# A planned order with later places, and another beginning: induced attention and a squared-ReLU layer on one core

## The chip, the cores and the metric

The kernel runs on one core of a Trainium2 chip. The metric is the device time of one execution in microseconds (us); the time before is the median of three runs. TensorE (PE) multiplies and transposes, ScalarE (ACT) and VectorE (DVE) work on what it leaves in PSUM and in SBUF, GpSimd (POOL) does some elementwise steps, and SyncE (SP) issues every DMA.

## What is computed

The input `x` has 4 batches of 12480 rows of 128 numbers, `inducing` 32 rows of 128. The two weights are float64: 128 x 2048 and 2048 x 128.

```python
def mab(q, kv):
    s = scale * (q @ kv.transpose(0, 2, 1))
    s = s - s.max(-1, keepdims=True)
    a = np.exp(s)
    a /= a.sum(-1, keepdims=True) + 1e-09
    return a @ kv
h = mab(I, x)                     # 32 inducing rows look at a whole batch
x2 = mab(x, h).reshape(-1, 128)   # each row looks at the 32 results
h = np.maximum(x2 @ w_in, 0.0)
out = h * h @ w_out
```

## The kernel before, in words

A batch is cut into 13 units of 960 rows (`NU`), a unit into two blocks of 480 columns (`BLK`); there are 52 units. Three kinds of work exist.

**First** (class `First`, L356) is the first attention of one unit: load it (L369), transpose it on PE (`xtp`, L388) and copy it to `xt`, scores against the inducing rows (`score`, L403), maximum and running shift on DVE (L416, L422), exponential on ACT (L429, L432), transpose the weights of the attention (`ep`, L437) and copy them to `et`, multiply with `xn` (`mix`, L457), and add up the running sum (`hacc` L469, `zs` L479). `first_end` (L509) closes a batch: it joins four groups of lanes into `hT`, multiplies it with the first weight in four pieces (`wp`, L559), and splits that into `hw` (L563, L568).

**Second** (L590) is the second attention of a unit: scores (`na`, L599), copy (`ss`), transpose (`s2t`, L616), maximum and subtraction (L623, L627), exponential (L630), a high and a low part `sk` (L649, L653), sum and reciprocal square (L634, L637, L640, L644: the last gives `zz`), transpose back (`ap`, L660), copy (`sw`) and four DMAs that spread it (`st<-sw`, L675).

**The layer** (`ffn_block`, L734) runs over quads of four 128-wide slices of the hidden size: four products `h` (L755) into two PSUM tiles of two banks, two ReLUs (L763) into `g`, one square (L774), a high part `hi` (L778) and a low part `lo` (L782) on DVE, and twelve products into `op` (L795). A unit has 8 quads, so 32 products `h` and 96 products `op`. At the end of a block `op` is copied (`ot`), transposed (`otp`, L815), scaled by `zz` (L823) and, for each unit, stored.

The weights come as float64 words in eight chunks of 512 KB (`weights`, L235; four of the first weight, `i0` to `i3`, four of the second, `o0` to `o3`). A chunk goes through `clamp` (L254, DVE), `size` (L260, ACT), `flush` (L263), `field` (L267), `sign` (L273), `power` (L279), `low` (L283, all DVE); then a chunk of the first weight has one sum on POOL (L322), one of the second a copy on ACT (L339) and two steps on POOL (L343, L344).

The order of all this is not written by hand. `Plan.run` (L66) is a list scheduler: each task has an engine, an assumed duration, a due time and needs; a task may start when its needs have ended plus `LATENCY` of the engine that did them, and when its buffers are free (their last user's end plus 60 ns, L98). Among tasks that could start within 40 ns of the engine's being free, the one due first is taken (L112). The plan sets only the order in which each engine's instructions are emitted: on the chip each engine runs its queue in that order and waits for semaphores where it must. SP's loads are ordered in the same way. The first batch has all 13 units of `First` done ahead of the layer, with no layer to hide behind (L846 to L857); in the other batches `First`, `Second` and the layer of different units are mixed. The task `opened` (L856) opens the memory of `g`, `hi` and `lo` where the weights' and the first units' tiles were; all ReLUs of unit 0 need it.

Of the kernel before, what the change touches and what calls it, by code (L numbers as in the profile page):

```python
# [20 lines left out]
P = 128  # L21
TS = 120
# [5 lines left out]
class Task:  # L28
    def __init__(self, engine, ns, fn, due, needs, port, mode, takes, order):
        self.engine, self.ns, self.fn, self.due = engine, ns, fn, due  # L30
        self.needs, self.port, self.mode, self.takes, self.order = needs, port, mode, takes, order
        self.start = self.end = self.ready = None
        self.waiting = 0
        self.then = []
# [9 lines left out]
class Plan:  # L44
# [7 lines left out]
    LATENCY = {"PE": 220.0, "ACT": 150.0, "DVE": 150.0, "POOL": 150.0, "SP": 2500.0}  # L52
    SWITCH = 95.0

    def __init__(self, room):
        self.room, self.tasks = room, []

    def add(self, engine, ns, fn, due, needs=(), port=False, mode=None, takes=(), reads=()):

        t = Task(engine.split("|"), ns, fn, due, [n for n in needs if n is not None], port, mode, takes, len(self.tasks))  # L60
        for b in list(takes) + list(reads):
            b.users.append(t)
        self.tasks.append(t)
        return t

    def run(self):  # L66
# [20 lines left out]
        def room_at(t):  # L87
            at = 0.0
            n = {}
            for b in t.takes:  # L90
                n[b.tag] = n.get(b.tag, 0) + 1
                old = taken.get(b.tag, [])
                i = len(old) + n[b.tag] - 1 - self.room[b.tag]
                if i >= 0:
                    for u in (old[i].users if i < len(old) else ()):
                        if u.end is None:
                            return None
                        at = max(at, u.end + 60.0)  # L98
            return at
# [42 lines left out]
def induced_attention_then_squared_relu_ffn(  # L142
# [19 lines left out]
    PERIOD, START, T_MAIN, NARROW, STEP = 32000.0, 2600.0, 66000.0, 6000.0, 1700.0  # L162
    W_DUE = [8000.0 + 6500.0 * k for k in range(8)]

    XT, OT, ST, SKH = ("ACT|DVE", "ACT|DVE"), ("ACT|DVE", "ACT|DVE"), "ACT|DVE", "ACT|DVE"
# [11 lines left out]
    plan = Plan(dict(xn=3, early=6, xt=NU + 1, m=2, h=2, o=2, g=GB, hi=HB, lo=LB, st=2, sw=2, words=2))  # L177
# [54 lines left out]
    LEAST = float(np.array(897 << 20, np.int32).view(np.float32))  # L232
    ABOVE = float(np.array(1151 << 20, np.int32).view(np.float32))

    def weights(name, load, use, due):  # L235

# [15 lines left out]
        def clamp():  # L252
            v["hc"] = tile_of("hc", F32)
            nc.vector.tensor_scalar(  # L254
                v["hc"], v["w"][:, :, 1].bitcast(F32), ABOVE, -ABOVE, ALU.min, ALU.max
            )

        def size():
            v["m"] = tile_of("m", F32)
            nc.scalar.activation(v["m"], v["hc"], AF.Abs)  # L260

        def flush():
            nc.vector.scalar_tensor_tensor(v["hc"], v["m"], LEAST, v["hc"], ALU.is_ge, ALU.mult)  # L263

        def field():
            v["a"] = tile_of("a", I32)
            nc.vector.tensor_scalar(  # L267
                v["a"], v["hc"].bitcast(I32), 3, 0x3FFFFFF8,
                ALU.logical_shift_left, ALU.bitwise_and,
            )  # L270

        def sign():
            nc.vector.scalar_tensor_tensor(  # L273
                v["a"], v["hc"].bitcast(I32), -0x40000000, v["a"], ALU.bitwise_and, ALU.bitwise_or
            )

        def power():
            v["power"] = tile_of("m", I32)
            nc.vector.tensor_single_scalar(v["power"], v["a"], -0x800000, ALU.bitwise_and)  # L279

        def low():
            v["b"] = tile_of("b", F32)
            nc.vector.scalar_tensor_tensor(  # L283
                v["b"], v["w"][:, :, 0].bitcast(U32), 2.0 ** -52, v["power"].bitcast(F32),
# [15 lines left out]
    def open_stage():  # L300
        pools["scope"] = ExitStack()
        pools["early"] = pools["scope"].enter_context(tc.tile_pool(name="early", bufs=6))
        pools["stage"] = pools["scope"].enter_context(tc.tile_pool(name="stage", bufs=2))

    def open_ffn():

        pools["scope"].close()
        pools["ffn"] = ctx.enter_context(tc.tile_pool(name="ffn", bufs=3))

    def load_weights(due):  # L310
# [3 lines left out]
        for k in range(n):  # L314
# [5 lines left out]
            def use(v, needs, due, kw, sl=sl):  # L320
                def join():
                    nc.gpsimd.tensor_add(w_in_sb[:, sl], v["a"].bitcast(F32), v["b"])  # L322

                return add("POOL", 1100, join, due, needs, **kw)

            ins.append(weights(f"i{k}", load, use, due[k]))
        for k in range(n):
# [6 lines left out]
            def use(v, needs, due, kw, k=k):  # L334
# [6 lines left out]
                def rest():  # L341
                    a = v["a"].bitcast(F32)
                    nc.gpsimd.tensor_sub(a, a, hi)  # L343
                    nc.gpsimd.tensor_add(lo, a, v["b"])  # L344
# [11 lines left out]
    class First:  # L356
        def __init__(self, b, u, due, early=False):

            self.b, self.u, self.early, self.n = b, u, early, f"{b}_{u}"
# [11 lines left out]
            loaded = add("SP", 2000, load, due - lead - (4000 if early else 20000), takes=[self.bx])  # L371
# [4 lines left out]
        def turn(self, k, due, loaded):  # L376
# [18 lines left out]
            t = add("PE", 420, turn, due, [loaded] + self.turned,  # L395
# [89 lines left out]
    def first_alone(f, due):  # L485

        v = {}
        bank_s, bank_h = Buffer("h"), Buffer("m")

        def score():  # L490
            v["sp"] = ps_h.tile([P, 2, 512], F32, tag="h", name=f"sp_{f.n}")[:, 0, :2 * TS]
            f.score(v["sp"])

        t = add("PE", 560, score, due, f.turned, mode="n", takes=[bank_s], reads=[f.bt])
        f.weigh(t, lambda: v["sp"], bank_s, due)
        mix_alone(f, due + 4000)

# [11 lines left out]
    def first_end(b, due, step):  # L509
# [46 lines left out]
        def wide(k):  # L556
            sl = slice(k * 512, (k + 1) * 512)
            v["wp", k] = bank(f"wp_{b}_{k}")
# [23 lines left out]
        for k in range(F // 512):  # L582
            bw = Buffer("m")
# [6 lines left out]
    class Second:  # L590
# [13 lines left out]
        def weigh(self, scored, where, bank_, due, step):  # L604
# [31 lines left out]
            def norm1():  # L636
                nc.vector.tensor_scalar_add(v["z"], v["z"], 1e-9)  # L637

            def norm2():
                nc.vector.reciprocal(v["z"], v["z"])  # L640

            def norm3():
                s["zz", u] = tiny.tile([TS, G, 1], F32, tag="zz", name=f"zz_{n}")
                nc.vector.tensor_mul(s["zz", u], v["z"], v["z"])  # L644


            def high():
                v["sk"] = att.tile([TS, Q, 2, 2, M], F32R, tag="sk", name=f"sk_{n}")
                copy(th, v["sk"][:, :, :, 0, :], v["d"].rearrange("t (k q) m -> t q k m", q=Q))  # L649
# [33 lines left out]
            d = due  # L683
            te = add("DVE", 317, evict, d, [scored], reads=[bank_])
# [4 lines left out]
            th = add(SKH, (300, 250), high, d + 3 * step, [tp], port=True)  # L689
            tl = add("DVE", 335, low, d + 3 * step, [th], port=True)  # L690
            t = add("DVE", 330, total, d + 4 * step, [tp])
            t = add("DVE", 75, norm1, d + 5 * step, [t])
            t = add("DVE", 113, norm2, d + 5 * step, [t])
            self.zz = add("DVE", 198, norm3, d + 5 * step, [t])
# [4 lines left out]
    def narrow(second, f, g, due, step, begun=None):  # L699

        v = {}
        bank_a = Buffer("m") if second or f else None
# [9 lines left out]
        def go():  # L712
            if bank_a:
# [20 lines left out]
    def ffn_block(b, u, k, second, t0, first_needs):  # L734
# [7 lines left out]
        def quad(j, last):  # L742
# [4 lines left out]
            for i in range(2):  # L747
# [12 lines left out]
                def relu(i=i, c=c):  # L760
                    if i == 0:
                        v["g"] = pools["ffn"].tile([P, 4, BLK], F32, tag="g", name=f"g_{n}_{j}", bufs=GB)
# [4 lines left out]
                t = add("PE", 217, lambda wide=wide: wide(0), d, need, takes=[bh], reads=[second.bst])  # L767
                w.setdefault("begun", t)
                t = add("PE", 217, lambda wide=wide: wide(1), d, [t], reads=[bh, second.bst])
                relus.append(add("ACT", 855, relu, d + 1000, [t] + first_needs + relus,  # L770
# [5 lines left out]
            def high():  # L776
                v["hi"] = pools["ffn"].tile([P, 4, BLK], F32R, tag="hi", name=f"hi_{n}_{j}", bufs=HB)
                nc.vector.tensor_copy(v["hi"], v["g"])  # L778

            def low():  # L780
                v["lo"] = pools["ffn"].tile([P, 4, BLK], F32R, tag="lo", name=f"lo_{n}_{j}", bufs=LB)
                nc.vector.tensor_sub(v["lo"], v["g"], v["hi"])  # L782

            sq = add("ACT", 1696, square, due + 4000, relus, reads=[bg])
            th = add("DVE", 1070, high, due + 5700, [sq], port=True, takes=[bhi], reads=[bg])
            tl = add("DVE", 2076, low, due + 7800, [th], port=True, takes=[blo], reads=[bg, bhi])
            for m, (wo, name, from_, buf) in enumerate((
                (wo_hi, "hi", th, bhi), (wo_lo, "hi", th, bhi), (wo_hi, "lo", tl, blo),
            )):
                for i in range(2):  # L790
# [10 lines left out]
                    last = add("PE", 434, products, due + 8000 + 600 * (2 * m + i), [from_, last, w_outs[j]],  # L801
# [32 lines left out]
        td = add(OT[k], (455, 570), done, end + 1000, [last], reads=[bo])  # L834
# [14 lines left out]
    t_end = 6000 + START * NU + 4000  # L849
# [3 lines left out]
    firsts[NU] = First(1, 0, t_main)  # L853
    narrow(seconds[0], None, None, t_end + 4000, 800)
    after_stage = w_ins + w_outs + [firsts[NU - 1].summed]
    opened = add("POOL", 1, open_ffn, t_main, after_stage)  # L856
    narrow(None, firsts[NU], None, t_main, 2000)  # L857
    open_stage()
    for w, (b, u) in enumerate(units):
        t_u = t_main + w * PERIOD  # L860
        begun = [ffn_block(b, u, k, seconds[w], t_u + k * PERIOD / 2, [opened] if w == 0 else []) for k in range(2)][0]
# [50 lines left out]
```

## Time and profile before

| | before |
|---|---|
| median of 3 runs | 1776.12 us (1775.27 to 1777.15) |
| the profiled execution's own time | 1777.57 us |
| its span, first to last instruction | 1775.8 us |
| mean granted clock of TensorE | 0.993 |
| busy share of PE, DVE, ACT, POOL | 98%, 92%, 93%, 1% |

The busy shares are averages over two very different parts: a beginning of some 72 us in which only the first attention of batch 0 and the weights are done, and a long part in which the layer runs. A row of the timeline has start, duration, engine, line, operation, out<-in, shape and count, and in brackets the idle time ahead of it with what ended it. The chain of waits lists, in order of time, what each stretch of the span was spent on, followed back from the last instruction.

### The profile page before, as it was taken

What the parts mean: (1) busy time and instruction counts of PE and PEld (TensorE: products, weight loads), DVE (VectorE), ACT (ScalarE), POOL (GpSimd) and SP (SyncE); (2) the same over time, 40 slices, a digit from 0 to 9 for tenths busy, and PEclk for the clock granted to TensorE, in tenths of its full rate; (3) what the DMA queues carried; (4) which work ended last, traced back from release to release, by engine and by line L of the source; (5) the groups of instructions that cost most, each with busy time, mean ns of one, the idle gap of its engine ahead of it and who ended that gap; (6) DMA issues with size and microseconds to landing.
All of it is one profiled execution on the core that took longest, in us unless ns stands there. A gap on an engine that the chain in (4) does not pass through costs nothing.

```text
span 1775.8 us, 24582 instructions
## 1 busy us (share of the span) xinstructions
PE 1736.6 (98%) x9625; PEld 1415.7 (80%) x9625; DVE 1641.0 (92%) x1736; ACT 1652.7 (93%) x1765; POOL 22.2 (1%) x22
## 2 busy tenths in 40 slices
PE   7799999999999999999999999999999999999998
PEld 4488888888788888888888888888887788888886
DVE  6799999999999999999999999999999998999988
ACT  6699999999999999999999999999999999999997
POOL 1200000000000000000000000000000000000000
PEclk9899999999999999999999999999999999999999
DMA  9211211211121211211211211111101001010110
GB/s 234 62 45 45 56 34 45 56 35 44 34 56 45 56 37 43 56 45 36 59 29 45 56 45 38 52 46 48 31 23 42 26 23 45 23 45 23 35 33 23
DMA packets 33532, 82.48 MB, mean 46 GB/s; under 512 B 5032, under 2 KB 20424, under 8 KB 33416
## 3 DMA queue, kind: packets, MB, share of 16 engines
q1 hardware_dynamic: 33416, 80.91, 17.4%
q8 instruction: 76, 1.25, 0.3%
q14 instruction: 40, 0.33, 0.1%
HBM read 29.77 MB, written 25.56 MB: 31 GB/s over the span
## 4 chain that ended last, share of the span: by engine, by line
PE 67%; ACT 20%; issue 9%; DVE 2%; DMA 1%; SPq 0%; ACTq 0%; DVEq 0%
PE op L795 43%; PE h L755 15%; ACT g L763 13%; ACT g L774 6%; PE otp L815 2%; PE xtp L388 1%; PE ap L660 1%; PE na L599 1%; DMA xn<-in_x_dram 1%; PE wp L559 1%; PE s2t L616 1%; PE na L403 1%; DVE lo L782 1%; PE ep L437 1%; ACT xt L224 1%
## 5 line engine op out<-in xcount | busy, mean ns | idle before, releaser
L782 DVE TENSOR_TENSOR lo<-g,hi 128x1920 fp32r<-128x1920 f32 x416 | 895.6, 2153 | 13.0 <-DVE hi L778 0.9
L763 ACT ACTIVATE g<-h 128x960 f32<-128x960 f32 x832 | 783.0, 982 | 47.8 <-PE h L755 42.1
L774 ACT ACTIVATE g<-g 128x1920 f32<-128x1920 f32 x416 | 759.4, 1826 | 5.1
L755 PE MATMUL h<-st,hw 128*128 128x480 f32 x1664 | 644.3, 388 | 15.4 <-ACT g L763 12.5
L778 DVE CAST hi<-g 128x1920 fp32r<-128x1920 f32 x416 | 480.1, 1154 | 78.8 <-ACT g L774 75.3
L795 PE MATMUL op<-lo,wo_hi 128*128 128x480 f32 x1664 | 511.1, 389 | 0.3 <-DVE lo L782 0.3
L795 PE MATMUL op<-hi,wo_lo 128*128 128x480 f32 x1664 | 506.0, 390 | 0.0
L795 PE MATMUL op<-hi,wo_hi 128*128 128x480 f32 x1664 | 481.8, 382 | 0.2 <-DVE hi L778 0.2
L755 PEld LDWEIGHTS h<-st,hw 128*128 128x128 f32 x1664 | 314.3, 189 | 108.3 <-ACT g L763 55.7
L795 PEld LDWEIGHTS op<-hi,wo_hi 128*128 128x128 f32 x1664 | 311.4, 188 | 50.3 <-DVE hi L778 0.9
L795 PEld LDWEIGHTS op<-hi,wo_lo 128*128 128x128 f32 x1664 | 299.6, 188 | 50.6 <-issue 11.7
L795 PEld LDWEIGHTS op<-lo,wo_hi 128*128 128x128 f32 x1664 | 302.2, 189 | 40.4 <-issue 2.7
L224 ACT COPY ot<-op 128x480 f32<-128x480 f32 x99 | 55.8, 564 | 27.1 <-PE op L795 26.9
L823 DVE TENSOR_TENSOR osb<-otp,zz 120x512 f32<-120x512 f32 x104 | 71.2, 684 | 4.2 <-PE otp L815 2.5
L388 PE MATMUL xtp<-ident,xn 120*128 120x120 f32 x416 | 62.7, 278 | 7.3 <-DMA xn<-in_x_dram 5.4
L388 PEld LDWEIGHTS xtp<-ident,xn 120*128 120x128 f32 x416 | 51.0, 147 | 21.0 <-issue 6.2
L815 PE MATMUL otp<-ident,ot 128*120 128x128 f32 x416 | 62.4, 272 | 0.6 <-ACT ot L224 0.6
L815 PEld LDWEIGHTS otp<-ident,ot 128*120 128x120 f32 x416 | 48.9, 137 | 15.6 <-ACT ot L224 6.6
L224 ACT COPY xt<-xtp 128x480 f32<-128x480 f32 x66 | 36.3, 555 | 13.7 <-PE xtp L388 13.6
L660 PEld LDWEIGHTS ap<-identr,sk 120*128 120x128 f32 x208 | 31.5, 193 | 4.8 <-DVE hw L568 1.5
L599 PE MATMUL na<-xt,hT 128*32 128x240 f32 x416 | 32.3, 382 | 0.0
L660 PE MATMUL ap<-identr,sk 120*128 120x120 f32 x208 | 29.5, 265 | 0.0
(95 smaller groups left out, 673.9 us busy)
## 6 DMA issues: line engine op xcount, KB each, us to landing
xn<-in_x_dram SPq DMA_DIRECT2D x52, 480.0 KB, 4.3
st<-sw SPq DMA_DIRECT2D x208, 120.0 KB, 2.6
out_dram<-osb SPq DMA_DIRECT2D x52, 480.0 KB, 3.5
words_i<-in_moe_w_in_dram SPq DMA_DIRECT2D x4, 512.0 KB, 10.3
words_o<-in_moe_w_out_dram SPq DMA_DIRECT2D x4, 512.0 KB, 7.5
ind_sb<-in_inducing_dram SPq DMA_DIRECT2D x1, 16.0 KB, 1.8
```

Source lines behind the costliest of these rows:

```text
L224: ENG[task.by](dst, src)
L388: nc.tensor.transpose(v["tp"][:, t * TS:(t + 1) * TS], self.xn[:, 4 * k + t, :], ident[:TS, :TS])
L599: nc.tensor.matmul(where[q * M:(q + 1) * M, :], self.s["hT"][:, :M], self.s["xt"][self.u][:, q * 2 * TS:(q + 1) * 2 * TS], start=True, sto ...
L660: nc.tensor.matmul(ap[:, q * TS:(q + 1) * TS], v["sk"][:, q].rearrange("t k a m -> t (k a m)"), identr[:TS, :TS], start=(q == 0), stop=(q ...
L755: nc.tensor.matmul(c["hp"][:, l, :BLK], s["hw"][:, f * P:(f + 1) * P], s["st", u][:, k, :], start=True, stop=True,)
L763: nc.scalar.activation(v["g"][:, 2 * i:2 * i + 2, :], c["hp"][:, :, :BLK], AF.Relu)
L774: nc.scalar.activation(v["g"], v["g"], AF.Square)
L778: nc.vector.tensor_copy(v["hi"], v["g"])
L782: nc.vector.tensor_sub(v["lo"], v["g"], v["hi"])
L795: nc.tensor.matmul(w["op"][:, :BLK], wo[:, 4 * j + l, :], v[name][:, l, :], start=(j == m == l == 0), stop=(j == NQ - 1 and m == 2 and l = ...
L815: nc.tensor.transpose(tp[:TS, q * P:(q + 1) * P], w["ot"][:, q * TS:(q + 1) * TS], ident)
L823: nc.vector.tensor_mul(s["osb", u].rearrange("t (q k) c -> t k q c", k=2)[:, k], w["tp"][:TS, :].rearrange("t (q c) -> t q c", q=Q), s["zz ...
```

## The change

- **Later places.** Each task has a margin `late` (200 ns for PE tasks, 100 ns for others, from `T_MAIN` on; 150 ns for the products `h`, 400 for the copy `ot`, 0 for ReLU, square and `lo`) that is added to the latency of its needs and to the release of its buffers; that release is counted with 100 ns instead of 60. A PE task that needs a PE task has no latency any more (220 before). Some assumed durations are slightly longer.
- **Smaller changes of work in every unit.** The 1e-9 and the square of the second attention's sum go from DVE to POOL, and DVE takes the reciprocal after them; the high part `sk` is always on DVE.
- **Weights.** `size` (ACT) comes first and reads the loaded words, one `clamp` follows, `flush` is gone, and the steps that POOL did are DVE's. `words` has three buffers, not two. Chunks of the second weight are due at 42 to 48 us, but their loads 20 us before that, at 22 to 28 us.
- **First batch.** The scores of unit u and the mix of unit u-2 form one group on PE. `wp` of batch 0 uses the PSUM tiles of `h`. The first `Second` writes `st` by two groups of PE with doubled columns and two copies, without the four DMAs. The first unit of batch 1 waits for the first piece of `hw`. `g` needs only the first units' tiles to be free; `hi` waits for all weights. `T_MAIN` is 60 us, 66 before.

```diff
-    LATENCY = {"PE": 220.0, "ACT": 150.0, "DVE": 150.0, "POOL": 150.0, "SP": 2500.0}
+    LATENCY = {"PE": 220.0, "ACT": 150.0, "DVE": 185.0, "POOL": 150.0, "SP": 2500.0}
+    LATE = {"PE": 200.0, "other": 100.0}
...
+            late = self.LATE["PE" if engine == "PE" else "other"] if due > self.begin else 0.0
...
-            t.ready = max([n.end + self.LATENCY[n.by] for n in t.needs], default=0.0)
+            for n in t.needs:
+                own = n.by == "PE" and t.engine == ["PE"]
+                t.ready = max(t.ready, n.end + (0.0 if own else self.LATENCY[n.by] + t.late))
...
-                        at = max(at, u.end + 60.0)
+                        at = max(at, u.end + 100.0 + t.late)
...
-    W_DUE = [8000.0 + 6500.0 * k for k in range(8)]
+    W_DUE = [10000.0, 16000.0, 22000.0, 28000.0, 42000.0, 44000.0, 46000.0, 48000.0]
+    LATE_G1, LATE_OT = 150.0, 400.0
...
-        t = add("SP", 2100, words, due - 6000, takes=[buf])
+        t = add("SP", 2100, words, due - 6000 if due < 40000 else due - 20000, takes=[buf], late=0)
+        t = add("ACT", 540, size, due, [t], **kw)
         t = add("DVE", 340, clamp, due, [t], port=True, **kw)
-        t = add("ACT", 530, size, due, [t], **kw)
-        t = add("DVE", 700, flush, due, [t], port=True, **kw)
...
-                return add("POOL", 1100, join, due, needs, **kw)
+                return add("DVE", 600, join, due, needs, port=True, **kw)
...
-                return add("POOL", 2300, rest, due, [t], **kw)
+                t = add("DVE", 600, rest, due, [t], port=True, **kw)
+                return add("DVE", 600, join, due, [t], port=True, **kw)
...
             def norm1():
-                nc.vector.tensor_scalar_add(v["z"], v["z"], 1e-9)
+                nc.gpsimd.tensor_scalar(v["z"], v["z"], 1e-9, 0.0, ALU.add, ALU.add)
 
             def norm2():
-                nc.vector.reciprocal(v["z"], v["z"])
+                v["zz"] = tiny.tile([TS, G, 1], F32, tag="z3", name=f"z3_{n}")
+                nc.gpsimd.tensor_mul(v["zz"], v["z"], v["z"])
 
             def norm3():
-                nc.vector.tensor_mul(s["zz", u], v["z"], v["z"])
+                nc.vector.reciprocal(s["zz", u], v["zz"])
...
-                t = add("PE", 217, lambda wide=wide: wide(0), d, need, takes=[bh], reads=[second.bst])
+                t = add("PE", 219, lambda wide=wide: wide(0), d, need, takes=[bh], reads=[second.bst], late=LATE_G1)
...
-                relus.append(add("ACT", 855, relu, d + 1000, [t] + first_needs + relus,
+                relus.append(add("ACT", 864, relu, d + 1000, [t] + g_open + relus, late=0,
...
-            th = add("DVE", 1070, high, due + 5700, [sq], port=True, takes=[bhi], reads=[bg])
+            th = add("DVE", 1070, high, due + 5700, [sq] + parts_open, port=True, late=200, takes=[bhi], reads=[bg])
...
-        first_alone(firsts[u], 6000 + START * u)
+        narrow(None, firsts[u], firsts[u - 2] if u > 1 else None, 6000 + START * u, 0, early=True)
...
-    firsts[NU] = First(1, 0, t_main)
+    firsts[NU] = First(1, 0, t_main + 6000, begun=state[0]["wide"][0])
```

## Rows read from the trace of the kernel before

**Rows 1.** The page's first part: busy time, share of the span, instructions.
```profile
PE 1736.6 (98%) x9625; PEld 1415.7 (80%) x9625; DVE 1641.0 (92%) x1736; ACT 1652.7 (93%) x1765; POOL 22.2 (1%) x22
```
**Rows 2.** Busy time by stretch: length, PE, PEld, DVE, ACT, POOL, clock, DMA, GB/s.
```profile
0.00:71.65 71.65, 52.63 (x497) 31.17 (x497) 50.33 (x127) 40.84 (x105) 15.85 (x18) 0.89 0.70 174
111.37:472.00 360.63, 357.74 (x2014) 296.28 (x2013) 338.43 (x356) 342.49 (x362) 2.20 (x1) 1.00 0.17 46
```
**Rows 3.** PE's waits from 84 us on: total us, times, longest.
```profile
PE h L755 <- ACT g L763: 11.7, 43, 0.3
```
**Rows 4.** PE's timeline around one such wait, in the unit from 242 to 275.
```profile
271.18 0.60 PE L795 MATMUL op<-lo,wo_hi 128*128 128x480 f32 x2
272.08 0.49 PE L755 MATMUL h<-st,hw 128*128 128x480 f32 x1 [0.29 <-ACT g L763]
```
**Rows 5.** The chain of waits: the same place of two neighbouring units.
```profile
339.00 2.16 PE op L795 x10
371.85 2.19 PE op L795 x10
```
**Rows 6.** SP's timeline from 28 to 45 us: the loads' issue.
```profile
29.26 0.40 SPq L329 DMA_DIRECT2D words_o<-in_moe_w_out_dram  x1
31.72 2.38 SPq L369 DMA_DIRECT2D xn<-in_x_dram  x2
37.54 1.40 SPq L369 DMA_DIRECT2D xn<-in_x_dram  x3
```
**Rows 7.** Issues from 33 to 35 us, the last of batch 0's loads: us to landing.
```profile
xn<-in_x_dram SPq DMA_DIRECT2D x1, 480.0 KB, 7.9
```
**Rows 8.** Busy time by stretch of ten us, same columns as rows 2.
```profile
30.00:40.00 10.00, 8.59 (x120) 5.42 (x118) 8.24 (x23) 7.55 (x23) 1.31 (x1) 1.00 0.99 236
60.00:70.00 10.00, 6.84 (x19) 3.74 (x17) 8.42 (x16) 3.65 (x8) 2.61 (x2) 0.61 0.01 3
```
**Rows 9.** The chain of waits in the beginning: start, us, what.
```profile
49.94 1.22 DVE zs L479
59.80 1.78 DVE b_o L283
63.24 3.75 PE wp L559 x4
66.99 1.06 PE ap L660 x4
69.23 2.31 DMA st<-sw
71.68 1.55 PE h L755 x3
```
**Rows 10.** The timeline at the same time, on POOL.
```profile
49.43 1.71 POOL L343 TENSOR_TENSOR a_o<-a_o,wo_hi 128x512 f32<-128x512 f32 x1 [2.94 <-DVE hacc L469]
```
**Rows 11.** DVE's and POOL's groups from 0 to 73.4 us: busy us, mean ns, idle before.
```profile
L479 DVE SCALAR_TENSOR_TENSOR zs<-zs,fade,z 128x1 f32<-128x1 f32 x11 | 6.5, 590 | 0.0
L283 DVE SCALAR_TENSOR_TENSOR b_o<-words_o,m_o 128x512 f32<-128x512 uint32 x4 | 3.8, 960 | 0.1
L263 DVE SCALAR_TENSOR_TENSOR hc_i<-m_i,hc_i 128x512 f32<-128x512 f32 x4 | 2.8, 693 | 1.9 <-ACT m_i L260 1.9
L254 DVE TENSOR_SCALAR hc_i<-words_i 128x512 f32<-128x512 f32 x4 | 1.7, 426 | 6.0 <-DMA words_i<-in_moe_w_in_dram 6.0
L479 DVE SCALAR_TENSOR_TENSOR zs<-z,fade,z 128x1 f32<-128x1 f32 x1 | 0.2, 216 | 0.0
L537 POOL TENSOR_SCALAR sums<-ones,zs 128x128 f32<-128x128 f32 x1 | 0.4, 376 | 0.1
```
**Rows 12.** ACT's and DVE's groups from 111 to 472 us, same columns.
```profile
L224 ACT CAST sk<-d 120x256 fp32r<-120x256 f32 x11 | 4.5, 409 | 0.3
L782 DVE TENSOR_TENSOR lo<-g,hi 128x1920 fp32r<-128x1920 f32 x89 | 191.6, 2153 | 2.6 <-DVE hi L778 0.5
L778 DVE CAST hi<-g 128x1920 fp32r<-128x1920 f32 x88 | 101.6, 1155 | 17.0 <-ACT g L774 16.7
```

More of the change, by code (lines that the diff above doesn't have):

```diff
@@ L28, with __init__ @@
 class Task:
-    def __init__(self, engine, ns, fn, due, needs, port, mode, takes, order):
+    def __init__(self, engine, ns, fn, due, needs, port, mode, takes, late, order):
         self.engine, self.ns, self.fn, self.due = engine, ns, fn, due
-        self.needs, self.port, self.mode, self.takes, self.order = needs, port, mode, takes, order
+        self.needs, self.port, self.mode, self.takes = needs, port, mode, takes
+        self.late, self.order = late, order
         self.start = self.end = self.ready = None
@@ L50, with __init__, add @@
     ENGINES = ("PE", "ACT", "DVE", "POOL", "SP")
-    LATENCY = {"PE": 220.0, "ACT": 150.0, "DVE": 150.0, "POOL": 150.0, "SP": 2500.0}
+    LATENCY = {"PE": 220.0, "ACT": 150.0, "DVE": 185.0, "POOL": 150.0, "SP": 2500.0}
     SWITCH = 95.0
[L55 to L60, printed above, removed]
+    LATE = {"PE": 200.0, "other": 100.0}
+    def __init__(self, room, begin):
+        self.room, self.begin, self.tasks = room, begin, []
+    def add(self, engine, ns, fn, due, needs=(), port=False, mode=None, takes=(), reads=(), late=None):
+        if late is None:
+            late = self.LATE["PE" if engine == "PE" else "other"] if due > self.begin else 0.0
+        needs = [n for n in needs if n is not None]
+        t = Task(engine.split("|"), ns, fn, due, needs, port, mode, takes, late, len(self.tasks))
         for b in list(takes) + list(reads):
@@ L369, in load @@
                 nc.sync.dma_start(self.xn, x_v[b, :, u * NT:(u + 1) * NT, :])
-            loaded = add("SP", 2000, load, due - lead - (4000 if early else 20000), takes=[self.bx])
+            loaded = add("SP", 2000, load, due - lead - (4000 if early else 20000), takes=[self.bx], late=0)
             self.turned = []
@@ L483, in add_up @@
             s["summed"] = self
[L485 to L496, printed above, removed]
     def mix_alone(f, due):
@@ L688, in weigh @@
             tp = add("ACT", 307, power, d + 2 * step, [td])
-            th = add(SKH, (300, 250), high, d + 3 * step, [tp], port=True)
-            tl = add("DVE", 335, low, d + 3 * step, [th], port=True)
-            t = add("DVE", 330, total, d + 4 * step, [tp])
-            t = add("DVE", 75, norm1, d + 5 * step, [t])
-            t = add("DVE", 113, norm2, d + 5 * step, [t])
-            self.zz = add("DVE", 198, norm3, d + 5 * step, [t])
+            if first:
+                t = add("DVE", 420, high1, d + 3 * step, [tp], port=True)
+                tl = add("DVE", 670, low1, d + 3 * step, [t], port=True)
+            else:
+                th = add("DVE", 210, high, d + 3 * step, [tp], port=True)
+                tl = add("DVE", 335, low, d + 3 * step, [th], port=True)
+            t = add("DVE", 330, total, d + 4 * step, [tp])
+            t = add("POOL", 150, norm1, d + 5 * step, [t])
+            t = add("POOL", 150, norm2, d + 5 * step, [t])
+            self.zz = add("DVE", 120, norm3, d + 6 * step, [t])
+            if first:
+                t1, last = [], None
+                for k in range(2):
+                    ba = Buffer("m")
+                    t = add("PE", 460, lambda k=k: back1(k), d + 4 * step, [tl], takes=[ba])
+                    last = add(ST, (455, 565), lambda k=k: stacked1(k), d + 5 * step, [t, last],
+                               takes=[] if k else [self.bst], reads=[ba] + ([self.bst] if k else []))
+                    t1.append(last)
+                self.ready = last
+                return
             t = add("PE", 460, back, d + 4 * step, [tl], takes=[ba])
@@ L697, in weigh, with narrow @@
             self.ready = add("SP", 1000, spread, d + 6 * step, [ts], takes=[self.bst], reads=[bw])
-    def narrow(second, f, g, due, step, begun=None):
+    def narrow(second, f, g, due, step, begun=None, early=False):
         v = {}
-        bank_a = Buffer("m") if second or f else None
+        bank_a = Buffer("h" if early else "m") if second or f else None
         bank_b = Buffer("m") if g else None
@@ L833, in ffn_block @@
         end = t0 + PERIOD / 2 + 8000
-        td = add(OT[k], (455, 570), done, end + 1000, [last], reads=[bo])
+        td = add(OT[k], (455, 570), done, end + 1500, [last], reads=[bo], late=LATE_OT)
         t = add("PE", 420, turn, end + 3000, [td], takes=[bt])
```

124 lines of the change are left out of this document (76 added, 48 removed).

## Prediction, made before the change was run

> **What bounds the kernel now.** I read the busy shares first: PE has 98% of the span, ACT 93%, DVE 92% [rows 1]. A share of 98% says nothing about which stretch has room, so I then read the busy time by stretch [rows 2]. In the first 71.65 us PE is busy for 52.6, DVE for 50.3, ACT for 40.8: none is full, so this part is a chain of waits. In the eleven units from 111 to 472 us PE is busy for 357.7 of 360.6, DVE for 338.4, ACT for 342.5: PE bounds. How tightly, two views say. The same place of two neighbouring units is 32.85 us apart (371.85 - 339.00), and ten products `op` in a row take 2.16 us, so one takes 0.22 [rows 5]. PE's waits after the beginning are almost one kind only: `h` waits for the ReLU that empties its PSUM tile, 43 times, 11.7 us in all [rows 3], which is nearly one for each of the 51 units that remain. The timeline of PE shows one [rows 4]: two products begin at 271.18 and should be issued by 271.62, the next `h` begins at 272.08. So a hole costs 0.46 us, more than the 0.29 that the row calls idle, because the matmul before and after a hole overlap less. 43 holes are 20 us, and this is all that a better order can give in the long part: the rest of PE's time is products.
>
> The beginning is the other place. The last load of batch 0 is the second of the pair issued from 31.72 to 34.10, so at 33.8, and lands 7.9 us later, at 41.7 [rows 6, 7]. The DMA engines are 99% busy at 236 GB/s then [rows 8]: the first pass is fed as fast as the loads come. The first `h` begins at 71.68 [rows 9], 30 us after the landing, and in that stretch TensorE's granted clock falls to 0.61 on average (60 to 70 us), that is part of it at 1.2 GHz, while PE waits [rows 8].
>
> **The beginning, part by part.**
>
> (a) *Loads.* SP issues by due time. The loads of `o0` to `o3` become due at 22, 24, 26 and 28 us, those of the last three units of batch 0 at 25.5, 28.1 and 30.7 (6000 + 2600 u - 6500 ns). So far one chunk of the second weight went ahead of the last load (29.26), and three loads of batch 1 went behind it while it was on its way (37.54) [rows 6]. With three `words` buffers I count `o0`, `o1`, `o2` ahead of it, two more: 2 x 524 KB at 236 GB/s [rows 8] are 4.4 us. What shared the engines with it from 37.5 on moves behind; I give back 1.4. **+3**, bounds 0 and +6.6 (all four ahead).
>
> (b) *The chain from that landing to the first `h`.* VectorE's `zs` took 0.59 on average and 0.216 once, alone [rows 11]; the one at 49.94 took 1.22 [rows 9], and ended as a 128 x 512 step of POOL did, which ran from 49.43 for 1.71 [rows 10]. A second such follows on the chain. With POOL's weight steps gone: -2 x 1.0 = -2.0. `b_o` at 59.80 took 1.78 [rows 9], against 0.96 on average [rows 11], and loses 0.8 at least: -1.0. `flush` (0.69 each [rows 11]) is gone; two of them stand in the chain's way: -1.3. The transpose `ap` at 66.99 stands behind four `wp` of 3.75 [rows 9] whose tiles were `s2t`'s until then; with `wp` in other tiles I take half, -1.8 (0 to -3.75). The DMA of 2.31 and its issue of 0.5 [rows 9] give way to a second group of PE (1.06 at most, as `ap`), a second copy, a second cast and a second subtraction (some 0.4 to 0.6 each): -1.0. Against this two POOL steps for each chunk are now VectorE's, at 0.69 each, as `flush` was [rows 11]: four for two chunks between landing and `st`, +2.8 (0 to +6.8, a whole chunk more). Sum **-4.3**, bounds -9 and +2.
>
> (c) *VectorE as a bound.* A chunk of the first weight costs five steps less `flush` plus one sum, so no change; one of the second 0.69 more: +2.8 in all. The stretched steps give back 11 x (0.59 - 0.216) = 4.1 and 4 x (0.96 - 0.69) = 1.1 [rows 11]. 50.3 [rows 2] becomes some 48 of 70: not the bound, **0**; +1 if `hi` of unit 0 waits for the last chunk.
>
> (d) *A new wait.* ACT's `size` now meets the load first; until now VectorE's `clamp` did, with 6.0 us of idle time ahead of four [rows 11]. Behind it in ACT's queue are the copies of `xt` and the exponentials, for which PE waits. The larger part of the 6.0 is the first chunk's, ahead of all work; the first pass waits for loads anyhow: **0**, at most +1.5.
>
> (e) *Batch 1's first unit* goes behind the first piece of `hw`: eight transposes, the scores, two more transposes, 16 small products, with their copies and exponentials. In the filling of the layer PE has idle time for most of it: **+0.5** (0 to +2.3). Its load keeps its due time (38 us). The empty tasks that open memory go from POOL to SP and issue nothing; the ReLUs no longer wait for POOL: **-0.5**.
>
> The beginning: 3 - 4.3 + 0 + 0 + 0.5 - 0.5 = **-1.3**; from its bounds I keep -8 to +6, since not all of them fall to one side.
>
> **The long part.** The hole of a unit [rows 4] arises where the plan lets `h` follow the end of its ReLU by 60 ns. With 100 + 150 ns, and products that may now follow each other without 220 ns of assumed latency, the order puts one more pair of products (0.44) ahead of such an `h`. That pair fits the hole of 0.46. Also ACT, which is what `h` waits for, loses one cast of 0.409 per unit [rows 12] to VectorE, and VectorE gives two of its three tiny steps to POOL. A new order need not be free of holes: the bound below is all of them closed, -20, above the same once more, +20. I take 60% closed, since the reason for each hole is the one that the margin addresses: **-12**. The tail is unchanged.
>
> Sum: -1.3 - 12 = -13.3. The profiled execution took 1777.57 us for a span of 1775.8, 1.5 above the median; I put the difference on the median: 1776.1 - 13.3 = **1763**, and 1748 to 1770 for this case by itself (-20 - 8; -6 of the holes, 0).
>
> **A rule that speaks against it.** POOL now does two small steps in each unit while VectorE is busy for 94% of the time [rows 2], mostly with `lo` of 2.15 us and `hi` of 1.16 [rows 12]. In the beginning a VectorE step with two operands in SBUF (`zs`) was stretched from 0.216 to 0.59 on average beside POOL [rows 11]. The Trainium skill, SBUF — State Buffer, section "Who interferes with whom", says that GpSimd and VectorE share a port pair as an exclusive lock: a VectorE instruction with two SBUF inputs, or in a two-port mode, and a GpSimd instruction that reads SBUF block each other for the whole instruction, whoever is second. The stretched `zs` agrees; no row shows POOL beside `lo`.
>
> **Rivals.**
>
> 1. *The holes go elsewhere.* The two PSUM tiles of `h` stay as they are; an order that closes one hole may open another at the next ReLU. For it: ACT is at 95% [rows 2]. Time: 1776.1 - 1.3 = 1775, with the beginning's bounds 1768 to 1782.
> 2. *POOL holds VectorE up* (slower). A POOL step waits for the `lo` ahead of it (2.15), holds VectorE for its own length (0.376 at most, as `sums` [rows 11]), twice, and VectorE's reciprocal then waits for POOL. VectorE would lose up to 2.15 + 0.75 = 2.9 us in a unit. It has 16.7 / 11 = 1.5 us of waiting for ACT in a unit to spare [rows 12]; from there on PE waits for `hi`. The excess is 0 to 1.4; with half, 0.7 x 51 = +36 on 1763: 1799; with a quarter 1781.
> 3. *The loads bind.* All four chunks go ahead of the last unit's load (+6.6) and the chain shrinks by nothing; holes closed as forecast: 1776.1 + 6 - 12 = 1770. With the holes open it is 1782.
> 4. *It doesn't do what it says:* the order is not much later, since due times still decide among what is ready: 1775, as rival 1.
>
> **How the numbers follow.** Forecast 0.50; rivals 1 and 4 together 0.24; rival 2 0.14; rival 3 0.12 (two thirds of it with the holes closed). Two runs of this kernel can be told apart from some 0.2%, 3.6 us: 1772.6 to 1779.7 is no change. Faster: 0.50 + 0.07 of rival 1 + 0.07 of rival 3 = 0.64. Slower: 0.12 of rival 2 + 0.05 of rival 1 + 0.05 of rival 3 = 0.22. No change: 0.14. The range takes in the forecast's lower end and rival 2 at a third of its excess: 1748 to 1788.
>
> **What would show it.** In the profile after: the last load of batch 0 issued some 3 us later; `zs` at 0.21 throughout; no DMA ahead of the first `h`, and that `h` at 68 to 71; PE's waits for L763's ReLU at under half of 11.7 us; neighbouring units 32.6 apart. The prediction is wrong if a unit takes 32.9 or more, if VectorE waits for POOL at the reciprocal for over 1.5 us in a unit, or if the first `h` comes outside 64 to 78.

## Result, and the profile after

| | before | after |
|---|---|---|
| median | 1776.34 us (1775.27 to 1777.15, 4 runs) | 1752.23 us (1749.87 to 1754.33, 4 runs) |
| ratio, 95% interval | | 0.9864 [0.9847, 0.9881] |
| span of the profiled execution | 1775.8 us | 1752.5 us |
| first `h` / first product `op` | 71.7 / 78.6 us | 72.6 / 79.5 us |
| unit 0's last product begins at | 111.4 us | 113.6 us |
| distance of neighbouring units, batch 0 | 32.86 us | 32.31 us |
| the same in batch 3 | 31.23 us | 30.57 us |

A unit's end is the start of its 96th product `op` in the trace; the distances are means of nine (units 1 to 10, and nine units inside batch 3, which have no `First` work). The change is 24.1 us faster, 13.3 were forecast. The span falls by 23.3 us: up to the end of unit 0 the changed kernel loses 2.2 us, behind it it gains 25.4.

The first lines to read are PE's waits from 84 us on (total us, times, longest), the answer to [rows 3]. They are all there are:

```profile
PE op L843 <- DVE hi L826: 0.8, 1, 0.8
PE otp L863 <- ACT ot L238: 0.6, 1, 0.6
PE op L843 <- DVE lo L830: 0.5, 2, 0.3
```

The 43 waits of `h` for the ReLU are gone. The busy time by stretch (columns as [rows 2]), up to the first `h` and for the eleven units from unit 0's end on:

```profile
0.00:72.65 72.65, 48.51 (x492) 31.00 (x492) 47.36 (x130) 39.32 (x101) 1.88 (x9) 0.95 0.69 167
113.56:468.00 354.44, 354.44 (x2013) 297.12 (x2012) 344.29 (x358) 338.93 (x342) 28.26 (x23) 1.00 0.19 48
```

PE is busy for all of the long stretch. How it got there stands in the order. First the kernel before, PE's timeline some us ahead of [rows 4], then the kernel after, in the same unit:

```profile
262.83 0.59 PE L795 MATMUL op<-lo,wo_hi 128*128 128x480 f32 x2
263.26 0.38 PE L755 MATMUL h<-st,hw 128*128 128x480 f32 x1
263.49 0.59 PE L795 MATMUL op<-hi,wo_hi 128*128 128x480 f32 x2
263.92 0.38 PE L755 MATMUL h<-st,hw 128*128 128x480 f32 x1
```

```profile
272.11 0.60 PE L803 MATMUL h<-st,hw 128*128 128x480 f32 x2
272.56 0.60 PE L843 MATMUL op<-hi,wo_hi 128*128 128x480 f32 x2
272.99 1.04 PE L843 MATMUL op<-hi,wo_lo 128*128 128x480 f32 x4
273.86 0.60 PE L803 MATMUL h<-st,hw 128*128 128x480 f32 x2
274.30 1.04 PE L843 MATMUL op<-lo,wo_hi 128*128 128x480 f32 x4
```

Before, one `h` stands behind nearly every two products (I call this weaving below); from 150 to 430 us its products `op` come in 294 runs of two, 17 of four and 16 of ten, and all 276 `h` stand alone. After, the two `h` of a PSUM tile mostly come together (94 pairs, 59 `h` alone), and the products in 59 runs of two, 39 of four, 63 of six and 22 of eight. The time from the end of a ReLU to the first `h` of the next tile in the same place was 0.59 us at the median (tiles of units 2 to 9) and is 1.93.

Waits also stand where I didn't look, at PE's weight loads (PEld). Their waits from 111 to 472 us, of the kernel before and of the one after:

```profile
PEld h L755 <- ACT g L763: 10.9, 29, 0.7
```

```profile
PEld h L803 <- ACT g L811: 2.2, 11, 0.3
```

10.9 us in eleven units are 0.99 a unit; the PE rows of the same stretch show 2.9 us of idle time ahead of `h`. Neither is the loss itself. That is read from the starts: the distance from the start of the `h` or product before to the start of a tile's first `h`, less the 0.217 us that one takes in a row of them ([rows 5]), sums to 4.8 us in these eleven units, so some of the waiting of the weight loads cost nothing, and some of the loss is not called idle on PE. By this measure 43 of the 51 units before had a hole, the largest in each of 0.41 to 0.47 us, and the whole loss ahead of `h` is 24.5 us; after, no unit loses over 0.2 us there, and the whole is 2.8.

The beginning, some rows of the chain of waits after:

```profile
40.61 10.66 DMA words_o<-in_moe_w_out_dram
51.30 0.03 ACT m_o L269
51.86 0.54 ACT xt L238
57.87 0.75 POOL sums L540
61.55 2.07 PE wp L565 x2
70.97 0.64 PE ap L667 x4
71.64 0.57 ACT st L238
72.88 0.46 PE h L803 x2
```

The stretches of [rows 9] that I named are gone: no DMA ahead of the first `h`, no `wp` of 3.75 us in one piece. But the chain hangs on the last chunk's load, which lands at 51.3, and on a copy of `xt` that stood behind that chunk's first step in ACT's queue. The last load of batch 0, issued at 37.3, takes (us to landing)

```profile
xn<-in_x_dram SPq DMA_DIRECT2D x1, 480.0 KB, 10.7
```

and lands at 48.0, 6.4 us later than before ([rows 7]).

### The profile page after: what moved, and what is told of

It reads as the page before. It is cut to its first block, busy times and chain, and to the rows that moved or that the text cites. A ratio compares the mean times of both kernels' runs of the same rounds, so it can differ in the third digit from the quotient of the medians.

```text
span 1752.5 us, 24345 instructions
## 1 busy us (share of the span) xinstructions
PE 1719.0 (98%) x9629; PEld 1418.2 (81%) x9629; DVE 1662.6 (95%) x1726; ACT 1635.6 (93%) x1678; POOL 133.0 (8%) x114
## 4 chain that ended last, share of the span: by engine, by line
PE 96%; DMA 1%; DVE 1%; ACT 1%; issue 0%; POOL 0%; SPq 0%; DVEq 0%; ACTq 0%
PE op L843 63%; PE h L803 21%; PE otp L863 3%; PE xtp L404 2%; PE na L605 2%; DMA words_o<-in_moe_w_out_dram 1%; PE ap L691 1%; PE nb L473 1%; PE na L419 1%; PE wp L565 1%; PE s2t L622 1%; PE ep L453 1%; ACT g L811 0%; DMA xn<-in_x_dram 0%; PE sp L419 0%
## 5 line engine op out<-in xcount | busy, mean ns | idle before, releaser
L830 DVE TENSOR_TENSOR lo<-g,hi 128x1920 fp32r<-128x1920 f32 x416 | 895.5, 2153 | 18.5 <-PE h L803 0.5
L803 PE MATMUL h<-st,hw 128*128 128x480 f32 x1664 | 519.4, 385 | 0.9 <-ACT g L811 0.8
L843 PE MATMUL op<-lo,wo_hi 128*128 128x480 f32 x1664 | 470.9, 394 | 0.5 <-DVE lo L830 0.5
L843 PE MATMUL op<-hi,wo_lo 128*128 128x480 f32 x1664 | 432.3, 381 | 0.0
L803 PEld LDWEIGHTS h<-st,hw 128*128 128x128 f32 x1664 | 306.3, 188 | 63.9 <-ACT g L811 18.0
L843 PEld LDWEIGHTS op<-hi,wo_lo 128*128 128x128 f32 x1664 | 312.4, 188 | 51.1
L843 PEld LDWEIGHTS op<-lo,wo_hi 128*128 128x128 f32 x1664 | 293.4, 189 | 53.6 <-issue 11.4
L643 POOL TENSOR_SCALAR z<-z 120x8 f32<-120x8 f32 x52 | 89.6, 1723 | 1494.2 <-DVE z L640 1494.2
L647 POOL TENSOR_TENSOR z<-z 120x8 f32<-120x8 f32 x52 | 37.6, 723 | 4.3
L238 DVE COPY xt<-xtp 128x480 f32<-128x480 f32 x52 | 34.0, 654 | 0.7
L238 DVE COPY ot<-op 128x480 f32<-128x480 f32 x53 | 34.5, 651 | 0.0
```

The lines of the kernel that those rows point to most:

```text
L238: ENG[task.by](dst, src)
L643: nc.gpsimd.tensor_scalar(v["z"], v["z"], 1e-9, 0.0, ALU.add, ALU.add)
L647: nc.gpsimd.tensor_mul(v["zz"], v["z"], v["z"])
L803: nc.tensor.matmul(c["hp"][:, l, :BLK], s["hw"][:, f * P:(f + 1) * P], s["st", u][:, k, :], start=True, stop=True,)
L843: nc.tensor.matmul(w["op"][:, :BLK], wo[:, 4 * j + l, :], v[name][:, l, :], start=(j == m == l == 0), stop=(j == NQ - 1 and m == 2 and l = ...
```

## Experiments

All were timed in turns with the kernel before, whose median in these groups was 1776.9 to 1777.0 us. "Unit 0" is the end of unit 0, "units" the distance in batch 0, "batch 3" the distance there; these and the first `h` are from one profiled execution of each kernel. By "the long part" I mean the stretch from the end of unit 0 to the end of the span. e5 and e6 have two timed runs each.

| run | median us | ratio | first `h` | unit 0 | units | batch 3 |
|---|---|---|---|---|---|---|
| order alone (e1) | 1755.04 | 0.9882 [0.9866, 0.9899] | 73.3 | 112.5 | 32.31 | 30.41 |
| beginning alone (e2) | 1777.46 | 1.0003 [0.9993, 1.0012] | 71.8 | 111.4 | 32.88 | 31.22 |
| small work back (e3) | 1753.21 | 0.9869 [0.9855, 0.9884] | 70.8 | 112.5 | 32.34 | 30.42 |
| loads of the second weight late (e4) | 1752.89 | 0.9867 [0.9852, 0.9882] | 74.1 | 112.3 | 32.31 | 30.52 |
| no latency within PE, alone (e5) | 1754.95 | 0.9877 [0.9857, 0.9897] | 71.7 | 110.5 | 32.31 | 30.62 |
| margins alone (e6) | 1759.29 | 0.9901 [0.9882, 0.9921] | 72.6 | 113.4 | 32.34 | 30.90 |
| release of `h` alone (e7) | 1772.28 | 0.9976 [0.9965, 0.9987] | 71.1 | 111.0 | 32.88 | 30.84 |
| durations alone (e8) | 1782.68 | 1.0033 [1.0020, 1.0046] | 73.2 | 116.7 | 32.83 | 31.23 |
| batch 1's loads later in the plan (e9) | 1750.69 | 0.9856 [0.9840, 0.9873] | 69.1 | 110.0 | 32.31 | 30.53 |
| batch 1's loads wait (e10) | 1751.36 | 0.9855 [0.9840, 0.9870] | 70.1 | 111.0 | 32.29 | 30.57 |
| `size` later in ACT's queue (e11) | 1751.57 | 0.9855 [0.9840, 0.9870] | 73.1 | 111.9 | 32.30 | 30.55 |
| e10, e11 and e3 together (e12) | 1750.90 | 0.9856 [0.9839, 0.9872] | 70.9 | 109.9 | 32.29 | 30.42 |

### Which part gives the gain

**e1.** The kernel before with `late`, the new latencies and releases, the new durations and the later due time of the copy `ot`; nothing else.

> The kernel before with the later places and the new assumed durations alone; beginning, weights, first batch and the small steps of each unit are as before. Theory A (the margins close the hole of each unit, the small steps do nothing): units of batch 1 end 32.3 us apart as in the changed kernel, against 32.86 before; the end of unit 0 stays at 111 us; 1776 - 25 = 1751. Rival B (ACT is relieved by the cast and VectorE by the tiny steps, and that closes the holes): units stay at 32.7 to 32.9 and the time at 1772 to 1777.

Measured: -21.9 us, units at 32.31, and 25.4 us in the long part, as the changed kernel. All of the gain there comes from the order. Rival B falls.

**e2.** The changed kernel with the order's settings and each unit's small steps as before, so the new beginning alone.

> The kernel before with the new beginning alone (weights on VectorE, grouped first batch, st without DMA, T_MAIN 60); order settings and small steps of each unit as before. Theory A: the beginning by itself costs time, as the trace of the changed kernel shows (unit 0 ends at 113.6 against 111.4): the end of unit 0 at 113 to 114 and units 32.86 apart, 1776 + 2 = 1778. Rival C (the later places lengthen the beginning, and the new beginning alone would end unit 0 earlier): unit 0 ends at 105 to 109, 1770 to 1774.

Measured: no change; unit 0 ends at 111.4 as before. With the order's settings of before, the new beginning is worth nothing, neither the loss of 2 us that the profiled run of the changed kernel shows nor a gain. With the new settings it is the same: e1 and e3 below differ in the beginning alone, and both end unit 0 at 112.5.

**e3.** The changed kernel with this undone:

```diff
-                nc.gpsimd.tensor_scalar(v["z"], v["z"], 1e-9, 0.0, ALU.add, ALU.add)
+                nc.vector.tensor_scalar_add(v["z"], v["z"], 1e-9)
...
-                th = add("DVE", 210, high, d + 3 * step, [tp], port=True)
+                th = add("ACT|DVE", (300, 250), high, d + 3 * step, [tp], port=True)
```

> The changed kernel with the three tiny steps of each second attention on VectorE again, and the cast for the high part free to go to ACT again, as before. Theory A: within 2 us of the changed kernel, units 32.3 apart, since PE bounds and VectorE's and ACT's spare time covers both; POOL's busy time falls from 133 to under 10 us. Rival B: units go back towards 32.86, the time to 1765 or more. Rival D (POOL held VectorE up in the changed kernel): faster than it by 3 us or more.

Measured: 1.0 us from the changed kernel, inside both intervals, and the long part takes the same time. The small steps do nothing for the whole, either way; in batch 3 a unit without them is 0.15 us shorter (30.42, and 30.41 in e1, against 30.57). Whether POOL's steps or the cast on VectorE cost that was not tried.

### Which part of the order

**e5.** The kernel before with one rule changed:

```diff
-            t.ready = max([n.end + self.LATENCY[n.by] for n in t.needs], default=0.0)
+            for n in t.needs:
+                own = n.by == "PE" and t.engine == ["PE"]
+                t.ready = max(t.ready, n.end + (0.0 if own else self.LATENCY[n.by]))
```

> The kernel before with one rule changed: a PE task that needs a PE task has no assumed latency (220 ns before). Theory A1 (the margin at the ReLU closes the hole): the hole stays, units 32.8 to 32.9, 1774 to 1778. Rival A2 (the plan wove an h between every two pairs of products because it held the next product back by 220 ns, and that weaving makes the hole): units 32.3 to 32.5, 1750 to 1760.

**e6.** The kernel before with the margins alone, `n.end + self.LATENCY[n.by] + (0.0 if own else t.late)`; it also has the 185 ns of VectorE's latency, which e8 has too, and the later due time of `ot`.

> The kernel before with the margins alone: 200 ns for PE tasks, 100 ns for others, the special ones for h, ot, hi, lo, ReLU and square, 100 ns at the release of buffers; the assumed latency between PE tasks and the durations of the four main tasks are as before. Theory A1: units 32.3 to 32.5, 1750 to 1760. Rival A2: units 32.8 to 32.9, 1774 to 1778.

**e7.** The kernel before with the one number on which my forecast rested:

```diff
-                        at = max(at, u.end + 60.0)
+                        at = max(at, u.end + (250.0 if b.tag == "h" else 60.0))
```

> The kernel before with one number changed: the release of a PSUM tile of h is counted 250 ns after its ReLU's end, not 60. The prediction's own reason (h follows the ReLU too closely in the plan): one more pair of products goes ahead of such an h, units 32.4 to 32.5, 1755 to 1762. Rival: the hole is made elsewhere (ACT reaches that ReLU late for another reason), units 32.8 to 32.9, 1774 to 1778.

**e8.** The kernel before with the assumed durations alone (217 to 219, 434 to 438, 855 to 864, 1696 to 1706 ns and so on).

> The kernel before with the new assumed durations alone (219 and 438 ns for h and products, 864 and 1706 for ReLU and square, 2070, 440, 185 ns of VectorE's latency). Theory A2 (the assumed latency between PE tasks makes the weaving, and the weaving the hole): products still in pairs with one h between them, units 32.8 to 32.9, 1774 to 1778. Rival G (the hole comes from ACT falling behind its planned times by some 15 ns a step): units 32.3 to 32.5, 1750 to 1760.

Measured, of the 25.4 us of the long part: e5 gives 22.3, e6 21.7 (all of the gain in batch 0 and half of it in batch 3), e7 5.3 (none in batch 0), e8 0.2. So neither A1 nor A2 is right as it was put: each of two edits gives most of it, though e6 keeps the weaving (295 runs of two products). What the kernels without the hole have in common is the distance from a ReLU's end to the `h` that follows it: 1.93 us at the median in the changed kernel, 1.72 in e5, 1.01 in e6, but 0.59 in e7 as before. The loss ahead of `h`, by the starts, is 3.7 us in e5, 6.8 in e6 and 13.2 in e7, against 24.5 before. The weight loads show the same order, from 111 to 472 us; e5, e6, e7:

```profile
PEld h L758 <- ACT g L766: 2.2, 10, 0.5
```

```profile
PEld h L764 <- ACT g L772: 4.7, 19, 0.3
```

```profile
PEld h L755 <- ACT g L763: 9.3, 32, 0.5
```

They are no measure of the loss, though: e6's are twice e5's, for 0.03 us a unit. e7 is the instructive one: PE's own rows show no wait of `h` for a ReLU in that stretch any more, and the units are on average as far apart as before. Its weight loads still wait 9.3 us for the ReLU, in more and shorter pieces, and 2.4 for `hi` (0.2 before). By the starts it did close holes in batch 0: ahead of `h` a unit loses 0.27 us and not 0.47. But ahead of the products it loses as much more: 0.35 behind an `h` and 0.74 behind a product, against 0.26 and 0.65. The mean also hides that its units are 33.3 and 32.35 us apart by turns. This is rival 1 of the prediction, the hole going elsewhere, for that edit alone. In batch 3 it did gain 0.4 us a unit. e8's unit 0 ends 5.3 us later and its units are as before: a few ns in the plan's assumed durations, and 35 ns of VectorE's latency, put the beginning into another order.

Which of e6's margins works was not tried, nor why the order without the 220 ns is free of the holes: that the weaving makes them is not shown, since e6 weaves without them.

### What sets the beginning

**e4.** `due - 6000` for the loads of all chunks.

> The changed kernel with one number changed: the loads of the second weight are due 6 us ahead of their conversion, like the first weight's, not 20. One chunk of the second weight then goes ahead of batch 0's last load, not three. Theory A (the last load of batch 0 sets the beginning): it lands 4 us earlier (at 43 to 44, not 47 to 48), the first h begins at 68 to 70, not 72.6, and unit 0 ends 2 to 4 us earlier: 1748 to 1750. Rival E (the last chunk of the weights sets it, through hi of unit 0): the first h earlier, but the first product op not, and 1751 to 1754.

Measured: the last load of batch 0 is issued 2.1 us earlier (35.2 against 37.3) and takes 6.9 us, not 10.7:

```profile
xn<-in_x_dram SPq DMA_DIRECT2D x1, 480.0 KB, 6.9
```

So it lands at 42.1, 5.9 us earlier than in the changed kernel, and still the first `h` comes 1.4 us later: theory A falls, the landing of that load by itself does not set the first `h`. A chunk's load issued at 37.11 now lands at 51.3 and holds ACT up, and the last chunk lands at 54.2 (51.3 in the changed kernel). The time is that of the changed kernel; rival E's sign for `h` was wrong, its time was right.

**e9.** In the plan, batch 1's loads need the copy of batch 0's last transposes.

> The changed kernel with batch 1's loads waiting for the copy of batch 0's last transposes; so batch 0's last load and the last weights have the DMA engines to themselves. Theory E2 (in the beginning all loads together bind, 13 + 3 units and 8 chunks, and three loads that nobody needs yet take 1.5 MB, 6 us, of it): the last unit's load lands 2 to 4 us earlier, the last chunk 4 to 6 us earlier, the first h begins at 68 to 70 and unit 0 ends at 109 to 111, not 113.6: 1747 to 1750. Rival F (the chain behind the last load binds, not the loads): first h within 1 us of 72.6, 1751 to 1754.

The edit changes the plan only; on the chip nothing makes the loads wait, and SP issued them 1.6 us earlier than the changed kernel did (41.05):

```profile
39.48 1.40 SPq L385 DMA_DIRECT2D xn<-in_x_dram  x3
```

So the 3.6 us by which unit 0 ends earlier can't be put down to held loads. Nor need the 1.6 us be the edit's: e3, whose beginning is the changed kernel's but for the small steps, issued them at 39.47. In e10 the loads really wait.

**e10.** The same with a one-column copy ahead of each such load:

```diff
+                if b == 1 and u < 3:
+                    nc.gpsimd.tensor_copy(self.xn[:, 0, :1], state["last_xt"].xt[:TS, UNIT - 1:UNIT])
                 nc.sync.dma_start(self.xn, x_v[b, :, u * NT:(u + 1) * NT, :])
```

> The changed kernel with batch 1's first three loads really waiting for batch 0's last unit: a one-column copy on GpSimd from that unit's xt into the tile ahead of each load (the loads overwrite it). Theory E2 (all loads together bind the beginning, and these 1.5 MB take 4 to 6 us of it): the last unit's load and the last chunk land 3 to 5 us earlier than in the changed kernel, and unit 0 ends at 108 to 111: 1747 to 1751. Rival F (the chain behind binds): unit 0 ends at 112.5 to 114, 1751 to 1754.

SP's timeline, and the busy time from 40 to 50 us:

```profile
49.44 1.24 SPq L387 DMA_DIRECT2D xn<-in_x_dram  x3
```

```profile
40.00:50.00 10.00, 8.89 (x104) 5.92 (x100) 9.24 (x27) 7.59 (x21) 0.73 (x3) 0.81 0.46 106
```

The loads wait, and the DMA engines are half idle (0.46; 1.01 in the changed kernel). Batch 0's last load lands 2.2 us earlier than in the changed kernel and the last chunk 4.3, and unit 0 ends at 111.0, 2.6 us earlier; e9, where nothing was held, gained as much. So free DMA engines give no more than that. VectorE is busy for 9.24 of these 10 us, and TensorE's granted clock is 0.81 there, so part of it at 1.2 GHz (1.00 in e9, all at 2.4). That VectorE's conversions bind is argued from this row, not shown.

**e11.** `reads=[buf], late=4500` for `size`.

> The changed kernel with 4.5 us more of assumed latency between a chunk's load and its first step on ACT, so that this step stands later in ACT's queue. Theory D2 (ACT waits for loads there, 4.1 us in four waits, with copies of xt queued behind; the last such wait is on the chain): those waits fall under 1 us and unit 0 ends 1.5 to 2.5 us earlier, 1749 to 1751. Rival: the waits vanish but the last chunk's conversion is later by as much, and unit 0 ends within 1 us of 113.6.

ACT's waits up to 72 us, after and in e11:

```profile
ACT m_o L269 <- DMA words_o<-in_moe_w_out_dram: 4.1, 4, 1.9
```

```profile
ACT m_o L269 <- DMA words_o<-in_moe_w_out_dram: 1.6, 1, 1.6
```

The waits fall by 2.5 us, unit 0 ends 1.7 earlier, the first `h` comes 0.4 later. The order of the loads changed with it: batch 0's last load lands at 45.1 (48.0 in the changed kernel), the last chunk at 54.0 (51.3).

**e12** puts e10, e11 and e3 together.

> The changed kernel with both of these, and with the three tiny steps and the free cast as before (which ended batch 3's units 30.42 apart, not 30.57). If the parts add up: unit 0 ends at 107 to 110, the last batch's units 30.4 apart, 1744 to 1748. If loads and waits are one cause seen twice: 1747 to 1751.

The parts do not add up: 1750.9. Four variants of the beginning lie 0.7 to 1.5 us under the changed kernel, whose runs spread over 4.5 us; their intervals overlap with its own. A version clearly better than it was not found, and what binds its beginning stays open. One more caution: the profiled run of the changed kernel is the slowest of its four (1754.33), so its beginning may be shown some 2 us too long.

## Why the prediction was right, and where not

- **The time** lies in the range, near its lower end, and in part by luck: the long part alone went past the bound that I gave it, and the range holds because its lower end also had 8 us for a shorter beginning, which didn't come.
- **The long part** was forecast at -12 with a bound of -20; it gave -25.4. The place was right (one hole a unit, where `h` waits for the ReLU), and so were the price and the number: by the starts, 43 units have a hole of 0.41 to 0.47 us, against 43 times 0.46. The mis-sized terms are two. The share of 60% closed was a guess; the changed kernel closed all 43. And "all that a better order can give" was too small: PE's rows leave out what stands outside these places. In batch 3 a unit loses 0.73 us ahead of `h` before and 0.16 after, and the products right behind an `h` lose 13.1 us in the 51 units before and 4.7 after, while those behind another product lose somewhat more (36.7 and 42.1, with the second `h` of a tile).
- **The step behind it failed.** I said that the hole arises because the plan lets `h` follow its ReLU by 60 ns. e7 changes that alone: in batch 0 the loss ahead of `h` falls from 0.47 to 0.27 us a unit, the products lose as much more, and no time is gained. The 220 ns of assumed latency between PE tasks, which I named in a half-sentence, gives 22.3 of the 25.4 us by itself (e5), and the margins without it 21.7 (e6).
- **The relief of ACT and VectorE** that I counted in favour is worth nothing for the whole (e3).
- **The beginning** was forecast at -1.3; in the profiled run it cost 2.2, by e2, and by e1 beside e3, nothing. (a) I counted the order of the loads rightly (`o0`, `o1`, `o2` ahead of the last), but not the landing: that load was issued at 37.3 and landed at 48.0, 6.4 later than before, against +3 and a bound of +6.6. (b) From there to the first `h` are 24.6 us, 30.0 before; -4.3 forecast, -5.4 measured. VectorE's steps are as forecast:

```profile
L495 DVE SCALAR_TENSOR_TENSOR zs<-zs,fade,z 128x1 f32<-128x1 f32 x11 | 2.3, 213 | 0.0
L291 DVE SCALAR_TENSOR_TENSOR b_o<-words_o,m_o 128x512 f32<-128x512 uint32 x4 | 2.7, 686 | 0.0
```

  (c) VectorE is busy for 47.4 us, 48 forecast. (d) The new wait on ACT, which I put at nothing and at most 1.5, is on the chain, with 1.9 us ahead of the last chunk: a copy of `xt` at 51.86 behind the chunk that landed at 51.3. (e) From the first `h` to the end of unit 0 are 40.9 us, 39.7 before: +1.2, against +0.5 for batch 1's first unit and -0.5 for the ReLUs. That it goes with that unit having moved there was not tried alone.
- **Rival 2, POOL holding VectorE up,** did not come about, though its first half did. POOL's groups from 113 to 1700 us, and one of these steps with VectorE's at the same time:

```profile
L643 POOL TENSOR_SCALAR z<-z 120x8 f32<-120x8 f32 x50 | 88.0, 1760 | 1458.0 <-DVE z L640 1458.0
L647 POOL TENSOR_TENSOR z<-z 120x8 f32<-120x8 f32 x50 | 37.2, 744 | 4.2
```

```profile
251.40 2.15 DVE L830 TENSOR_TENSOR lo<-g,hi 128x1920 fp32r<-128x1920 f32 x1
253.46 1.16 DVE L826 CAST hi<-g 128x1920 fp32r<-128x1920 f32 x1
251.57 3.09 POOL L643 TENSOR_SCALAR z<-z 120x8 f32<-120x8 f32 x1 [31.78 <-DVE z L640]
254.74 0.20 POOL L647 TENSOR_TENSOR z<-z 120x8 f32<-120x8 f32 x1
```

  The first of POOL's two steps, eight numbers per partition, takes 1.76 us on average and up to 3.09, beside `hi` and `lo` that VectorE runs back to back; at 69.4, with VectorE on other work, it took 0.24. `lo` kept its 2153 ns, and none of VectorE's waits behind unit 0 names POOL. The Trainium skill (SBUF — State Buffer, "Who interferes with whom") says that the second of the two to issue waits for the whole instruction; the trace agrees for POOL, and here the step lasted past one instruction: it began under `lo` and ended at 254.66, when the `hi` behind it ended (254.62). The price I gave needed the reciprocal to wait, and the order had put it late enough.
- **Rival 3** went as far as its first half: the last load landed later by nearly the 6.6 us that it named, with three chunks ahead of it and not four, and the shorter chain took 5.4 of that back.

## What to carry to other kernels

Where PE seems full, read the waits of its weight loads and the distances of matmul starts as well as its idle time. Here 10.9 us of waiting stood at the weight loads where PE's rows showed 2.9, the starts gave 4.8, and an edit that cleared PE's rows in that stretch (e7) left its units as far apart as before. In a list scheduler, an assumed latency between tasks of one in-order engine is not a safe margin: in this plan it wove other work in between, and taking it away gave 1.2% (e5). That every such plan loses by it is not shown; margins at the ReLU gave nearly as much with the weaving left (e6). And in the beginning, where loads, VectorE's conversions and a chain lie close together, five edits moved a few us from one to the other, and none gave a time clearly under that of the changed kernel.

## What the runs showed of the hardware

A GpSimd step of 120 x 8 numbers took 0.24 us once in the beginning, and 1.76 us on average in the long part, where VectorE ran casts (1.15 us) and differences (2.15 us) of tiles in SBUF back to back. The delay fell on GpSimd alone in these places; in the kernel before, beside GpSimd's steps on the weights, it fell on VectorE too: `zs` took 0.590 us on average, and 0.213 in the changed kernel, where these steps are gone.
